# The head of a fused linear-attention and squared-ReLU kernel: 64-row transfers on a second queue and another order of the first matmuls

## The chip, the cores and the metric

The kernel runs on one core of a Trainium2 chip. The metric is the device time of one execution in microseconds (us); several runs are taken and their median is given.

## The reference

The input x has 2048 tokens of 448 features in bf16. Everything works on its layer norm. One branch is linear attention with 16 heads of 28 columns; the other is a dense layer of 1792 columns with a squared ReLU; the result is x plus their gated product.

```python
xn = _layernorm(x, axis=-1)                      # eps 1e-5
# A: linear attention
q, k, v = (xn @ wqkv) split into 16 heads of 28
phi = lambda t: jnp.where(t > 0, t + 1, jnp.exp(t)) + 1e-6
kv  = einsum("bhsd,bhse->bhde", phi(k), v)
z   = einsum("bhsd->bhd", phi(k))
o   = einsum(phi(q), kv) / (einsum(phi(q), z) + 1e-6)
s   = o @ wo
# B: squared ReLU
h = xn @ w1 + b1;  r = where(h > 0, h, 0);  out = (r * r) @ w2 + b2
return x + s * silu(out)
```

## The kernel before

The 2048 tokens are 16 tiles of 128, in 4 groups of 512. The 448 features are three full chunks of 128 rows and a rest of 64. The rest of each weight is loaded twice, into partitions 0 to 63 and 64 to 127, so that two matmuls with 64 rows each run side by side in the two halves of the array. A weight thus comes in one main transfer (`load_main`, chunks 0 to 2) and two 64-row transfers (`load_rest`, named chunk 3 and 4). w1 is cut by columns into 0 to 511 (`w10`), 512 to 1279 (`w11`) and 1280 to 1791 (`w12`), each with a main and two 64-row transfers.

The code first lists operations with what they read and write (`add`), and a planner (`schedule`, `one_pass`) then orders them. TensorE and SyncE keep the order in which the operations were listed; ScalarE, VectorE and GpSimd take what the planner's model has ready, the lowest `prio` (or latest permitted start) first, and operations with `alts` may go to another engine. The model has a duration for each operation and, for a transfer, an issue time (`dur`, 0.45) and a rate (250 bytes per ns in the first 13 us, then 330). It only decides orders; the waits in the program are semaphores. A transfer is issued by the engine that it is listed on, SyncE or ScalarE, and each engine issues one after the other.

The head is what happens before the long stream of matmuls. For each of the tiles 0 to 3: `bn_stats` (L483) and `bn_aggr` (L484) on VectorE give mean and variance, Ln and Exp on ScalarE (L491, L495) give the reciprocal standard deviation, and a tensor_scalar on VectorE (L525, for tile 0 L503 in two pieces) gives the normalized tile. TensorE transposes its three full chunks through PSUM (`pe_transpose`, L602), ScalarE or VectorE copies them to SBUF (L613, L612), and the rests of two tiles go together (`pe_transpose_rests`, L627, copied at L637) after VectorE or ScalarE has doubled the last 64 columns (`ln_twin`, L541 or L542). `k_part` (L801) multiplies a tile's three chunks with w_k, `k_rests` (L816) adds the rests of two tiles. `head_part(lo, fi)` (L829) multiplies three chunks of w1's block fi (0 or 1) with tiles lo and lo+1, and `head_rest` (L845) adds the rest and hands blocks 0 and 1 (H0.0, H0.1) over. `bias_cols` (L1234) transposes the bias b1 that `b1r` holds. `warm(n)` (L1219) issues n matmuls of 128 columns on zeros into a bank that nobody reads.

After the head the matmuls H0.2, H0.3 (columns in w10), then H0.4, H0.5 and on (L786) follow, then Q and K, the second layer G (L1109), and so on through the four groups, in an order that is written out by hand. `pe_four` runs four such units in two interleaved pairs: the first to run behind the head are the eight matmuls of H0.2 and H0.3, then those of H0.4 and H0.5, which need w11.

The squaring of the ReLU (L775 on VectorE, L776 on ScalarE) takes two blocks at a time; the ReLUs are at L764 (ScalarE) and L761 (VectorE). The normalized tiles of groups 1 to 3 are transposed on VectorE and by small transfers (`dve_transpose`), which SyncE issues and, for three of group 1, ScalarE.

Of the kernel before, what the change touches and what calls it, by code (L numbers as in the profile page):

```python
# [46 lines left out]
class Program:  # L47
# [6 lines left out]
    def add(self, eng, emit, reads=(), writes=(), dur=0.2, alts=(), nbytes=0, mode=None, label="", slow=1.0):  # L54
        op = Op(eng, emit, reads, writes, dur, alts, nbytes, mode, label)
        op.slow = slow
        for t in op.reads:
            op.raw.add(self.writer[t])
            self.readers.setdefault(t, []).append(op)
        for t in op.writes:  # L60
            w = self.writer.get(t)
            if w is not None and w is not op:
                op.deps.add(w)
            for r in self.readers.get(t, ()):
                if r is not op:
                    op.deps.add(r)
            self.writer[t] = op
            self.readers[t] = [r for r in self.readers.get(t, ()) if r is op]
        op.raw.discard(op)
        op.deps |= op.raw  # L70
        for d in op.deps:
            d.succ.append(op)
        self.ops.append(op)
        return op
# [23 lines left out]
    def one_pass(self):  # L98
# [50 lines left out]
        while n:  # L149
# [76 lines left out]
            if op.nbytes:  # L226
                free[e] = st + op.dur
                s2 = max(dma_free, st + 1.0)
                dma_free = s2 + op.nbytes * op.slow / (250e3 if s2 < 13.0 else 330e3)
                op.end = max(dma_free + 0.45, st + 1.8)  # L230
            else:
                op.end = st + du
                free[e] = op.end
                if e == "pe":
                    last_mode = op.mode
# [70 lines left out]
def bass_recurrent_scan__linear_attn_block__dense_activation_squared_relu__prompt_kernel(  # L306
    nc, A_x, A_wqkv, A_wo, B_x, B_w1, B_b1, B_w2, B_b2, out
):
    with ExitStack() as es:
# [115 lines left out]
        def dma(eng, dst, src, writes, nbytes, reads=(), dur=0.45, slow=1.0):  # L425
            return add(
                eng, lambda e, _: e.dma_start(dst, src), reads, writes, dur, nbytes=nbytes, label="dma" + str(writes[0]), slow=slow  # L427
            )

        def load_x(lo, hi, eng="sp"):  # L430
            dma(eng, x_tok[:, lo:hi, :], tiles(A_x, lo, hi), [("x", i) for i in range(lo, hi)], (hi - lo) * P * D * 2)

        def load_main(eng, w, src, name, lo, hi, c0=0, c1=3, off=0):
            dma(
                eng, w[:, c0:c1, lo:hi],
                src[128 * c0 : 128 * c1, off + lo : off + hi].rearrange("(c p) j -> p c j", p=P),
                [(name, c) for c in range(c0, c1)], 128 * (c1 - c0) * (hi - lo) * 2,
            )

        def load_rest(eng, w, src, name, lo, hi, off=0):  # L440
            for i in (0, 1):
                dma(
                    eng, w[64 * i : 64 * i + 64, 3, lo:hi], src[384:448, off + lo : off + hi], [(name, 3 + i)],
                    64 * (hi - lo) * 2,
                )

        wn = lambda name: [(name, i) for i in range(5)]
        HA = 2
        cuts = (0, 4 * P, 10 * P, F)
        load_x(0, 1)  # L450
        load_x(1, 2, "act")
        load_x(2, 4)
        load_main("sp", w_k, A_wqkv, "wk", 0, D, 0, 1, off=D)
        load_main("sp", w_k, A_wqkv, "wk", 0, D, 1, 3, off=D)
        load_rest("sp", w_k, A_wqkv, "wk", 0, D, off=D)
        dma("act", b1r[:, :], B_b1.rearrange("(f p) -> f p", p=P), ["b1r"], F * 2)
        for n, (lo, hi) in enumerate(zip(cuts, cuts[1:])):
            load_main("sp", w_1, B_w1, f"w1{n}", lo, hi)
            load_rest("sp", w_1, B_w1, f"w1{n}", lo, hi)
            if n == 1:  # L460
                load_x(4, 8)
        load_main("sp", w_q, A_wqkv, "wq", 0, D)
        load_rest("sp", w_q, A_wqkv, "wq", 0, D)
        add("act", lambda e, _: e.preload_act_table_set("natural_log_exp_and_others"), [], ["actw"], 1.3, label="table").prio = 1e6
        late_constants()

        def late_loads():
# [11 lines left out]
        def hp(si, k):  # L479
            return None if si > 3 else 5 * si + k - 25  # L480

        def ln_stats(si):
            add("dve", lambda e, _: e.bn_stats(st6[:, si, :], x_tok[:, si, :]), [("x", si)], [("st", si)], 0.61, label=f"bn{si}").prio = hp(si, 0)  # L483
            add("dve", lambda e, _: e.bn_aggr(mv[:, si, :], st6[:, si, :]), [("st", si)], [("mv", si)], 0.16, label=f"ag{si}").prio = hp(si, 1)  # L484

        def ln_rstd(lo, hi):
            c = slice(lo, hi)
# [7 lines left out]
                "act", lambda e, _: e.activation(out=rstd[:, c], in_=vep[:, c], func=AF.Exp, scale=-0.5),  # L495
                [("vep", i) for i in ts], [("rstd", i) for i in ts], 0.2, label=f"rs{lo}",
            ).prio = -40 + lo if hi - lo == 1 else None

        def ln_norm_first(si):
            for lo, hi, names in ((0, P, [("xf", si)]), (P, D, [("xn", si)])):  # L500
                add(
                    "dve",
                    lambda e, _, lo=lo, hi=hi: e.tensor_scalar(  # L503
                        out=xn[:, si, lo:hi], in0=x_tok[:, si, lo:hi], scalar1=mv[:, si, 0:1],
                        scalar2=rstd[:, si : si + 1], op0=ALU.subtract, op1=ALU.mult,
                    ),
                    [("x", si), ("mv", si), ("rstd", si)] + ([("xf", si)] if lo else []), names, 0.2 if lo == 0 else 0.33,
                    label=f"xn{si}.{lo}",
                ).prio = hp(si, 3 if lo == 0 else 4)

        def xn_cols(si, lo, hi):
            if si < 4 * SWAP:
# [81 lines left out]
        def pe_transpose(si, pieces):  # L594
            for lo, hi, eng in pieces:
                b = Buf("T")

                def f(e, _, lo=lo, hi=hi, b=b):
                    v = ps(b)[:, :].bitcast(bf)
                    last = None  # L600
                    for c in range(lo, hi):
                        last = e.transpose(v[:, (c - lo) * P : (c - lo + 1) * P], xn[:, si, c * P : (c + 1) * P], ident[:, :])  # L602
                    return last

                src = ("xf" if (si, hi) == (0, 1) else "xn", si)
                add("pe", f, [src, "ident"], [b], 0.0558 * (hi - lo), mode="128", label=f"T{si}.{lo}")

                def ev(e, eng, lo=lo, hi=hi, b=b):
                    src = ps(b)[:, 0 : 64 * (hi - lo)].bitcast(bf)
                    dst = xT[:, si, lo:hi, :].rearrange("p c k -> p (c k)")  # L610
                    if eng == "dve":
                        return e.tensor_copy(dst, src)  # L612
                    return e.activation(out=dst, in_=src, func=AF.Copy)  # L613

                n = hi - lo
                add(
                    eng, ev, [b], [("xT", si, c) for c in range(lo, hi)],
                    0.15 + 0.07 * n if eng == "dve" else 0.18 + 0.107 * n, label=f"eT{si}.{lo}",
                ).prio = -30
# [178 lines left out]
        def k_part(si, lo, hi):  # L798
            def f(e, _):
                for c in range(lo, hi):  # L800
                    last = e.matmul(  # L801
                        ps(k_head[si])[:, 0:D], xT[:, si, c, :], w_k[:, c, :], start=(c == 0), stop=False, skip_group_check=True
                    )
                return last

            add(
                "pe", f, [("wk", c) for c in range(lo, hi)] + [("xT", si, c) for c in range(lo, hi)] + ([k_head[si]] if lo else []),
                [k_head[si]], (hi - lo) * MM(D), mode="128", label=f"K{si}.{lo}",
            )
# [403 lines left out]
        def warm(n, after=()):  # L1213
            b = Buf("W")

            def f(e, _):
                last = None
                for _i in range(n):
                    last = e.matmul(ps(b)[:, 0:P], dum[:, 0:P], dum[:, 0:P], start=True, stop=True)  # L1219
                return last  # L1220

            add("pe", f, ["dum", *after], [b], n * 0.075, mode="128", label="warm")

        for i in range(4):
            ln_stats(i)
            ln_rstd(i, i + 1)
            (ln_norm if i else ln_norm_first)(i)
            if i % 2:
                ln_twin(i - 1, i + 1)

# [5 lines left out]
            )  # L1236
            add("act", lambda e, _: e.activation(out=b1f[:, :], in_=ps(bb)[:, 0 : NF // 2].bitcast(bf), func=AF.Copy), [bb], ["b1f"], 0.2, label="b1f")

        warm(35)
        warm(7, [("mv", 0)])  # L1240
        pe_transpose(0, ((0, 1, "act"), (1, 3, "dve")))
        k_part(0, 0, 1)
        warm(4)
        k_part(0, 1, 3)
        pe_transpose(1, ((0, 3, "act"),))
        warm(6)
        pe_transpose(2, ((0, 3, "dve"),))
        k_part(1, 0, 3)
        pe_transpose_rests(0)
        bias_cols()  # L1250
        head_part(0, 0)
        head_part(0, 1)
        pe_transpose(3, ((0, 3, "act"),))
        k_rests(0)
        pe_transpose_rests(2)
        head_part(2, 0)
        head_part(2, 1)
        head_rest(0)


        def ln(lo, hi):
            for si in range(lo, hi):
# [122 lines left out]
```

## Time and profile before

| | |
|---|---|
| median of 3 runs | 146.56 us (146.54 to 146.73) |
| the profiled execution | 147.21 us, span from first to last instruction 145.0 us |
| granted clock of TensorE | 1.00 over the span |
| TensorE, matmuls | 140.3 us busy, 97% of the span |
| VectorE | 102.2 us, 70% |
| ScalarE | 80.2 us, 55% |
| GpSimd | 6.6 us, 5% |
| chain that ended last | TensorE 88%, DMA 4%, SyncE's issues 4%, VectorE 1% |
| transfers | 12.89 MB, mean 89 GB/s; SyncE's queue 11.46 MB, ScalarE's 1.25 MB |

Busy times come from a profile of one execution. A busy TensorE is one whose matmuls overlap in the pipeline; its pace is read from the distance between starts. In the views, PE is TensorE, PEld its weight loads, DVE VectorE, ACT ScalarE, POOL GpSimd, SP SyncE; a q behind the engine marks its sequencer, which issues transfers. L427 is the line that issues every transfer, so transfers are told apart by the tensors that they name: `w` stands for w_1 and w_2. The time to landing is counted from the start of the issue.

### The profile page before, as it was taken

Reading aid. Unit: us, or ns where it says so; the run is one execution under the profiler, and the core shown is the slowest. Engines: PE = TensorE matmul, PEld = TensorE weight load, DVE = VectorE, ACT = ScalarE, POOL = GpSimd, SP = SyncE. Lnnn points to the kernel's source line nnn. Section 1 sums busy time; section 2 is a strip of 40 time slices with the busy share of each in tenths; the row PEclk is TensorE's granted clock in tenths of the full one; section 3 lists DMA queues with packets and bytes.
Section 4 is the critical chain, followed back from the end, with each engine's and each line's share of the span. In section 5 each row is a group of like instructions: output and inputs, shape, how many; then the busy total and the mean of one; then the engine's idle time right before and its main releaser. Section 6 shows DMA issues by size and latency. Waiting matters only on the chain.

```text
span 145.0 us, 3036 instructions
## 1 busy us (share of the span) xinstructions
PE 140.3 (97%) x1195; PEld 70.9 (49%) x1195; DVE 102.2 (70%) x222; ACT 80.2 (55%) x148; POOL 6.6 (5%) x40
## 2 busy tenths in 40 slices
PE   7998999999999999999999999999999999999991
PEld 7763444554444444444444444444547455555471
DVE  1945998889588799859778888962033736874874
ACT  3468897113688717597878468888328340302311
POOL 7900000000000000000000000000000000000000
PEclk9999999999999999999999999999999999999999
DMA  4799996469232100132100000000497000323032
GB/s 146 219 236 307 281 346 149 70 176 265 38 49 43 25 0 5 27 54 46 22 0 0 0 0 5 0 0 18 136 206 171 3 5 17 100 73 99 32 119 71
DMA packets 23515, 12.89 MB, mean 89 GB/s; under 512 B 14290, under 2 KB 22734, under 8 KB 23502
## 3 DMA queue, kind: packets, MB, share of 16 engines
q1 hardware_dynamic: 21842, 11.46, 31.0%
q10 hardware_dynamic: 1660, 1.25, 3.8%
q8 instruction: 9, 0.15, 0.4%
q14 instruction: 4, 0.03, 0.1%
HBM read 9.23 MB, written 1.90 MB: 77 GB/s over the span
## 4 chain that ended last, share of the span: by engine, by line
PE 88%; DMA 4%; SPq 4%; DVE 1%; issue 0%
PE pb L786 28%; PE pb L1109 19%; PE pb L1092 7%; PE pb L1184 7%; PE pb L887 6%; PE pb L729 6%; PE pb L739 6%; DMA w<-in_B_w_dram 4%; SPq L427 4%; PE pb L1149 3%; PE pb L866 1%; DVE gbuf L1173 1%; PE pb L893 1%; PE pb L1036 1%; PE pb L961 1%; PE pb L1062 1%
## 5 line engine op out<-in xcount | busy, mean ns | idle before, releaser
L786 PE MATMUL pb<-xT,w 64*128 64x512 bf16 x378 | 43.8, 377 | 0.5 <-DMA w<-in_B_w_dram 0.5
L764 ACT ACTIVATE r<-pb,b1f 128x512 bf16<-128x512 f32 x39 | 25.3, 685 | 16.1 <-PE pb L786 16.0
L786 PEld LDWEIGHTS pb<-xT,w 64*128 64x128 bf16 x378 | 18.0, 94 | 23.3 <-issue 1.1
L1109 PE MATMUL pb<-w,r 128*128 128x448 bf16 x140 | 27.7, 353 | 0.0
L1109 PEld LDWEIGHTS pb<-w,r 128*128 128x128 bf16 x140 | 13.1, 98 | 13.9 <-issue 1.2
L776 ACT ACTIVATE r<-r 128x1024 bf16<-128x1024 bf16 x17 | 17.8, 1061 | 0.7 <-DVE r L761 0.5
L761 DVE TENSOR_SCALAR r<-pb,b1f 128x512 bf16<-128x512 f32 x17 | 12.4, 744 | 6.0 <-PE pb L786 6.0
L1082 DVE TENSOR_TENSOR gbuf<-pb,b2b 128x448 bf16<-128x448 f32 x14 | 8.5, 617 | 5.6 <-PE pb L1109 4.1
L1204 DVE TENSOR_TENSOR gbuf<-pb,gbuf 128x448 bf16<-128x448 f32 x14 | 8.1, 618 | 6.1 <-PE pb L1184 6.1
L1092 PE MATMUL pb<-w,r 64*128 64x448 bf16 x112 | 11.8, 350 | 0.0
L729 PE MATMUL pb<-w_k,xT 64*128 64x448 bf16 x98 | 11.6, 349 | 0.0
L483 DVE BATCH_NORM_STATS2 st<-x_tok 128x6 f32<-128x448 bf16 x16 | 9.2, 609 | 3.2 <-DMA x_tok<-in_A_x_dram 3.2
L739 PE MATMUL pb<-xT,w_q 64*128 64x512 bf16 x84 | 11.0, 376 | 0.0
L1132 ACT ACTIVATE gbuf<-gbuf 128x448 bf16<-128x448 bf16 x14 | 7.0, 570 | 6.8 <-DVE gbuf L1082 5.9
L1184 PE MATMUL pb<-w_k,pqT 64*128 64x448 bf16 x96 | 10.6, 349 | 0.0
L1000 DVE TENSOR_TENSOR pqT<-pqT,xT 128x2048 bf16<-128x2048 bf16 x3 | 3.7, 1221 | 8.4 <-DMA xT<-scr 8.4
L887 PE MATMUL pb<-pk,xn 128*128 128x448 bf16 x48 | 9.6, 353 | 0.0
L719 DVE SCALAR_TENSOR_TENSOR pk<-pb,pk 128x448 bf16<-128x448 f32 x16 | 9.3, 616 | 0.1
L923 DVE TENSOR_TENSOR zacc<-zacc,pk 128x448 f32<-128x448 f32 x13 | 8.1, 620 | 0.2
L707 ACT ACTIVATE pk<-pb 128x448 bf16<-128x448 f32 x16 | 7.8, 545 | 0.6 <-PE pb L729 0.6
L1092 PEld LDWEIGHTS pb<-w,r 64*128 64x128 bf16 x112 | 5.4, 94 | 5.3 <-issue 0.4
L719 DVE SCALAR_TENSOR_TENSOR pqT<-pb,pqT 128x512 bf16<-128x512 f32 x12 | 7.7, 681 | 0.0
(99 smaller groups left out, 140.2 us busy)
## 6 DMA issues: line engine op xcount, KB each, us to landing
out_dram<-gbuf SPq DMA_DIRECT2D x15, 112.0 KB, 1.7
w<-in_B_w_dram SPq DMA_DIRECT2D x1, 1568.0 KB, 9.9
x_tok<-in_A_x_dram SPq DMA_DIRECT2D x3, 448.0 KB, 6.5
xT<-gbuf SPq DMA_DIRECT2D x32, 32.0 KB, 2.0
w<-in_B_w_dram SPq DMA_DIRECT2D x2, 384.0 KB, 5.9
xT<-scr SPq DMA_DIRECT2D x6, 112.0 KB
w<-in_B_w_dram SPq DMA_DIRECT2D x1, 576.0 KB, 6.6
xT<-scr ACTq DMA_DIRECT2D x5, 112.0 KB
```

Source lines behind the costliest of these rows:

```text
L483: add("dve", lambda e, _: e.bn_stats(st6[:, si, :], x_tok[:, si, :]), [("x", si)], [("st", si)], 0.61, label=f"bn{si}").prio = hp(si, 0)
L719: lambda e, _: e.scalar_tensor_tensor(out=slot, in0=ps(buf)[0:rows, 0:n], scalar=1.0 + 1e-6, in1=slot, op0=ALU.add, op1=ALU.max),
L729: return e.matmul(ps(b)[:, 0:D], x_tile(rows, si, c), w_k[rows, c, :], start=start, stop=stop)
L739: return e.matmul(ps(b)[:, 0:512], w_q[rows, c, m * P : (m + 1) * P], x_group(rows, g, c), start=start, stop=stop,)
L761: return e.tensor_scalar(out=slot, in0=ps(b)[:, 0:512], scalar1=b1f[:, fi : fi + 1], scalar2=0.0, op0=ALU.add, op1=ALU.max)
L764: return e.activation(out=slot, in_=ps(b)[:, 0:512], func=AF.Relu, bias=b1f[:, fi : fi + 1])
L776: return e.activation(out=both, in_=both, func=AF.Square)
L786: return e.matmul(ps(b)[:, 0:512], w_1[rows, c, fi * P : (fi + 1) * P], x_group(rows, g, c), start=start, stop=stop,)
L887: last = e.matmul(ps(b)[:, 0:D], xn_cols(si, c * P, (c + 1) * P), pk[:, si, :], start=(si == 0), stop=(si == NT - 1),)
L1092: return e.matmul(ps(b)[:, 0:D], r_cols(rows, fi, si), w_2[rows, fi, :], start=start, stop=stop)
L1109: last = e.matmul(ps(b)[:, 0:D], r_cols(slice(0, P), fi, si), w_2[:, fi, :], start=(fi == 0), stop=(fi == NF - 1),)
L1184: return e.matmul(ps(b)[:, 0:D], w, msb[rows, c, :], start=start, stop=stop)
```

## The change

- The planner's rate of the first 13 us is 280 instead of 250, and a 64-row transfer's issue time in the model is 0.58 instead of 0.45.
- x tile 1 is issued by SyncE, behind tile 0, not by ScalarE.
- w_k's main part is one transfer instead of two. Its two 64-row transfers are issued by ScalarE.
- Of w10's two 64-row transfers the first is issued by ScalarE. The bias b1r is issued by SyncE, behind w10, not by ScalarE.
- ScalarE's table load comes first on its engine, ahead of the transfers.
- `bn_aggr` of tiles 0 and 1 gets a higher priority, so that each follows its own `bn_stats`.
- The first tile is normalized whole; `ln_norm_first` is gone.
- The listed order of the first matmuls, with their dummy matmuls and the engines that copy the transposed tiles, is another.

```diff
-                dma_free = s2 + op.nbytes * op.slow / (250e3 if s2 < 13.0 else 330e3)
+                dma_free = s2 + op.nbytes * op.slow / (280e3 if s2 < 13.0 else 330e3)
...
         def load_rest(eng, w, src, name, lo, hi, off=0):
             for i in (0, 1):
                 dma(
-                    eng, w[64 * i : 64 * i + 64, 3, lo:hi], src[384:448, off + lo : off + hi], [(name, 3 + i)],
-                    64 * (hi - lo) * 2,
+                    eng if isinstance(eng, str) else eng[i], w[64 * i : 64 * i + 64, 3, lo:hi], src[384:448, off + lo : off + hi], [(name, 3 + i)],
+                    64 * (hi - lo) * 2, dur=0.58,
                 )
...
         load_x(0, 1)
-        load_x(1, 2, "act")
+        load_x(1, 2)
         load_x(2, 4)
-        load_main("sp", w_k, A_wqkv, "wk", 0, D, 0, 1, off=D)
-        load_main("sp", w_k, A_wqkv, "wk", 0, D, 1, 3, off=D)
-        load_rest("sp", w_k, A_wqkv, "wk", 0, D, off=D)
-        dma("act", b1r[:, :], B_b1.rearrange("(f p) -> f p", p=P), ["b1r"], F * 2)
+        load_main("sp", w_k, A_wqkv, "wk", 0, D, off=D)
+        load_rest("act", w_k, A_wqkv, "wk", 0, D, off=D)
         for n, (lo, hi) in enumerate(zip(cuts, cuts[1:])):
             load_main("sp", w_1, B_w1, f"w1{n}", lo, hi)
-            load_rest("sp", w_1, B_w1, f"w1{n}", lo, hi)
+            load_rest(("act", "sp") if n == 0 else "sp", w_1, B_w1, f"w1{n}", lo, hi)
+            if n == 0:
+                dma("sp", b1r[:, :], B_b1.rearrange("(f p) -> f p", p=P), ["b1r"], F * 2)
             if n == 1:
                 load_x(4, 8)
...
-        add("act", lambda e, _: e.preload_act_table_set("natural_log_exp_and_others"), [], ["actw"], 1.3, label="table").prio = 1e6
+        add("act", lambda e, _: e.preload_act_table_set("natural_log_exp_and_others"), [], ["actw"], 1.3, label="table").prio = -1e6
...
-            add("dve", lambda e, _: e.bn_aggr(mv[:, si, :], st6[:, si, :]), [("st", si)], [("mv", si)], 0.16, label=f"ag{si}").prio = hp(si, 1)
+            add("dve", lambda e, _: e.bn_aggr(mv[:, si, :], st6[:, si, :]), [("st", si)], [("mv", si)], 0.16, label=f"ag{si}").prio = hp(si, 1) if si > 1 else si - 29
...
-        def ln_norm_first(si):
...
-                src = ("xf" if (si, hi) == (0, 1) else "xn", si)
-                add("pe", f, [src, "ident"], [b], 0.0558 * (hi - lo), mode="128", label=f"T{si}.{lo}")
+                add("pe", f, [("xn", si), "ident"], [b], 0.0558 * (hi - lo), mode="128", label=f"T{si}.{lo}")
...
-            (ln_norm if i else ln_norm_first)(i)
+            ln_norm(i)
...
-        warm(35)
-        warm(7, [("mv", 0)])
-        pe_transpose(0, ((0, 1, "act"), (1, 3, "dve")))
-        k_part(0, 0, 1)
+        warm(31)
+        warm(9, [("mv", 0)])
+        pe_transpose(0, ((0, 3, "act"),))
+        warm(7)
+        pe_transpose(1, ((0, 3, "dve"),))
+        k_part(0, 0, 3)
+        pe_transpose_rests(0)
+        k_part(1, 0, 3)
+        head_part(0, 0)
+        pe_transpose(2, ((0, 3, "dve"),))
+        head_part(0, 1)
+        k_rests(0)
         warm(4)
-        k_part(0, 1, 3)
-        pe_transpose(1, ((0, 3, "act"),))
-        warm(6)
-        pe_transpose(2, ((0, 3, "dve"),))
-        k_part(1, 0, 3)
-        pe_transpose_rests(0)
+        pe_transpose(3, ((0, 3, "dve"),))
         bias_cols()
-        head_part(0, 0)
-        head_part(0, 1)
-        pe_transpose(3, ((0, 3, "act"),))
-        k_rests(0)
         pe_transpose_rests(2)
+        warm(4)
         head_part(2, 0)
         head_part(2, 1)
         head_rest(0)
```

More of the change, by code (lines that the diff above doesn't have):

```diff
@@ L497, in ln_rstd @@
             ).prio = -40 + lo if hi - lo == 1 else None
-        def ln_norm_first(si):
[L500 to L509, printed above, removed]
         def xn_cols(si, lo, hi):
```

## The prediction

> **What bounds the kernel now.** I read the chain of waits first, because it says which stretch sets the end. Its columns are start, length (both us), and what the chain passes through.
>
> ```profile
> 6.36 0.50 SPq L427
> 6.90 6.17 DMA w<-in_B_w_dram
> 13.07 0.05 issue
> 13.11 8.38 PE pb L786 x76
> ...
> 136.54 4.30 PE pb L1149 x28
> 140.87 0.43 DVE gbuf L1162
> ```
>
> Up to 6.90 us the chain is SyncE issuing one transfer after the other; then it is the flight of the second 64-row piece of w1's columns 512 to 1279, which lands at 13.07; from 13.11 to 140.87 it is TensorE without a break. So everything that precedes 13.11 counts only by when H0.4, the first matmul that needs those columns, can start. The waits of TensorE from 13 us to 141 us confirm it: one entry.
>
> ```profile
> PE pb L786 <- DMA w<-in_B_w_dram: 0.5, 1, 0.5
> ```
>
> The third view is the timeline of the head (start, length, engine, what, xcount, idle before).
>
> ```profile
> 0.81 0.86 SPq L427 DMA_DIRECT2D x_tok<-in_A_x_dram  x2
> 1.05 4.66 PE L1219 MATMUL pb<-dum 128*128 128x128 bf16 x42 [1.05 <-DVE dum L368]
> 1.26 0.67 ACTq L427 DMA_DIRECT2D b1r<-in_B_b_dram  x1
> 1.96 1.28 ACT L464 ACT_TABLE_LOAD   x1 [1.96 <-issue]
> 4.70 0.29 ACT L491 ACTIVATE vep<-mv,eps 128x1 f32<-128x1 f32 x1 [1.46 <-DVE mv L484]
> 5.64 0.79 PE L602 MATMUL pb<-ident,xn 128*128 128x128 bf16 x3
> 7.37 0.50 PE L1219 MATMUL pb<-dum 128*128 128x128 bf16 x6
> 8.55 0.39 DVE L525 TENSOR_SCALAR xn<-x_tok,mv,rstd 128x448 bf16<-128x448 bf16 x1
> 10.05 0.49 ACT L613 ACTIVATE xT<-pb 128x384 bf16<-128x384 bf16 x1 [0.58 <-PE pb L602]
> 10.60 0.83 PE L829 MATMUL pb<-xT,w 128*128 128x256 bf16 x6
> 11.58 1.03 PE L786 MATMUL pb<-xT,w 64*128 64x512 bf16 x8
> ```
>
> A second limit lies close behind the transfer. The head matmuls of tiles 2 and 3 (L829) start at 10.60, H0.2 follows at 11.58 and is through at 12.61: from 10.60 to where H0.4 could begin are 2.01 us. An earlier transfer alone therefore gains at most 0.50 us; more needs the chain through the four tiles to move too.
>
> The table by half microseconds (length, busy time of PE, PEld, DVE, ACT, POOL, clock, share of the DMA engines, GB/s) says how full the DMA engines are while that chain runs.
>
> ```profile
> 4.00:4.50 0.50, 0.50 (x8) 0.50 (x6) 0.47 (x2) 0.00 (x0) 0.50 (x6) 1.00 0.80 151
> 5.50:6.00 0.50, 0.42 (x4) 0.10 (x1) 0.46 (x3) 0.19 (x2) 0.50 (x3) 1.00 0.53 99
> 8.00:8.50 0.50, 0.50 (x5) 0.28 (x5) 0.22 (x1) 0.47 (x3) 0.00 (x0) 1.00 0.91 101
> ```
>
> At 5.5 they ran half empty: w1's first piece was issued only at 3.92. At 8.0 they were busy but slow: waiting data, not a missing issue.
>
> **The change part by part. The transfers.** In SyncE's queue ahead of the last piece of the second cut of w1, the change removes one of w_k's two main issues (0.48 with its gap), its two 64-row issues (0.62, 0.63) and one of w1's (0.54), and adds x tile 1 (0.46) and the bias b1r (0.67 and a gap on ScalarE, say 0.65 here). Net 2.27 - 1.11 = 1.16 us earlier: 6.90 becomes 5.74. If the landing follows the issue it comes at 11.9. If it follows only the filling of empty DMA time, the table gives the gain: the unfilled shares of the six slices from 3.5 to 6.5 (0.85, 0.80, 0.89, 0.77, 0.53, 0.74) come to 1.42 slices, 0.71 us, so 12.36. The two slow slices at 8.0 stay in both. The pessimistic end is the one starved slice alone, 0.47 x 0.5 = 0.24 us: 12.8. I take 12.1, between the first two, since both starved time and a late issue are visible in the rows.
>
> **ScalarE.** The table moves to 0.8 and ends at 2.1; three 64-row issues follow. Rows for an issue go from 0.42 to 0.67, so they end near 4.0 (3.4 to 4.2). Behind them wait Ln and Exp of tile 0, and behind these the normalization, the transpose and all of the head. bn_stats of tile 0 can start when x lands (0.81 + 2.3 = 3.1) and takes 0.59; with aggregation at once (0.17) the statistics are there at 3.9, against 4.6 when both tiles' bn_stats went first. So Ln starts at about 4.05 instead of 4.70, and the normalized tile, 0.57 us after Ln's start plus 0.42, is there at 5.05. The issues hide under the statistics of tile 0; without that cover each further 0.1 us of issuing would cost 0.1. The other engine's issues can stretch one: where ScalarE issued beside SyncE at 24.4, one SyncE issue took 1.21 instead of 0.61. With three ScalarE issues that long Ln would start at 5.8. From Ln to the second L829 were 5.9 us: shifted whole, 11.7, and the kernel 0.6 slower. But VectorE can do a bn_stats (0.59) in that wait, and T3 stood 0.7 us behind the first Ha, from 8.94 to 9.68, so I get 10.4 to 10.7 and a gain of 0.3 to 0.5 left.
>
> **VectorE.** Removed: the split of the first normalization (0.71 becomes 0.42) and the evacuation of half of tile 0 (0.29). Added: evacuations of tiles 1 and 3 (0.36 each; ScalarE did them in 0.49). Its list up to the normalization of tile 3 was 5.5 us of work from 3.30 and ended at 8.94. Now it is 5.5 - 0.29 - 0.29 + 0.36 = 5.3 from 3.1, with 0.2 more if the copy of the last columns comes here: 8.6 to 9.0 with the same small waits.
>
> **TensorE.** The first 42 dummy matmuls have a pitch of 0.106 us ((4.66 - 0.31) / 41), the six at 7.37 one of 0.056: its clock came up at about 6.3. The new order has 40 dummies, to 1.05 + 40 x 0.106 = 5.3, so T0 starts at 5.3 and not when its tile is ready; before 5.63. Then, at the slow pitch, T0 and 7 dummies (10 x 0.107): 6.4. At the fast one T1 0.17, three K matmuls of tile 0 at 0.19, two rests 0.2, K of tile 1 0.57: 7.9, with up to 0.4 for the evacuation of T1 in this sum or beside it. Ha0 (3 x 0.11), T2 0.2, Ha1 0.33, K rests 0.25, four dummies 0.22: 9.3, and T3 0.17: 9.5. w1's first cut must be there at 8.0; it landed at 8.2 from 3.92 and is now issued at about 2.6. The result of T3 passes to VectorE and back: 0.28 for the matmul's end and the semaphore, 0.36, 0.1: Ha0 for tiles 2 and 3 at 10.25. b1r's transpose, the rests and four dummies fit beside that. 10.25 + 2.01 = 12.26 for H0.4.
>
> **Sum.** H0.4 starts at the later of 12.1 and 12.3: 12.3 against 13.11, a gain of 0.8 us. Behind it nothing seems to turn late. The second half of G0's sum starts 26.9 and the last squaring ends 24.1; w2 lands at 22.7 and G0 starts 24.3; the transposed second group is in SBUF by about 31.5 and H1 starts at 35.0. Each has over 1.5 us. The profiled execution took 147.21 us (span 145.0 and 2.2 around it) and becomes 146.4; the median of the runs, 146.56, lies 0.65 below that execution, so 145.8.
>
> **The rivals.** *The transfers come hardly earlier.* One set of 16 DMA engines serves both queues; if only the starved slice is filled, w1 lands at 12.8 and the gain is 0.3: 146.3. For it: the slices at 8.0, slow at a full share. Against: the starvation from 3.5 to 6.0. The Trainium skill (DMA: Bandwidth & Descriptors, Issuing engines are not separate DMA queues) says that issuing from several engines saves only the sequencer's issue time. By that rule the result is this rival or the 1.16 us of the issues, as the issue or the data binds; the trace shows both, one after the other.
>
> *Both limits come better.* If TensorE's clock comes up by 5.3 rather than 6.3, the ten slow matmuls cost 0.5 less, H0.4 could start at 11.75, and w1 at 11.9 binds: gain 1.2, 145.3.
>
> *Slower: the clock comes up later.* The change replaces the run of 42 by 40 dummies and puts T1, which waits for a normalized tile, ahead of all K work. If TensorE idles there before 6.3 and stays at the slow pitch, the 2.9 us of work that I counted from 6.4 to 9.3 takes up to twice as long. Half of it slow is 1.45 us: H0.4 at 13.75, 0.65 late, 147.2; all of it, 148.7. It decides from 0.8 us of such lag. Against it: in the trace the clock came up although TensorE had been idle for 0.2 to 0.4 us just before T0's pieces. The Trainium skill (TensorE: Matmul & The Clock Gate, Part 1) states that a free-running window of about 3.4 us must be busy for the clock to be released; the trace's 5.2 us from the first matmul to the fast pitch does not contradict that.
>
> *The gain is given back.* The change also alters the planner's rate and issue lengths, so the order on ScalarE and VectorE and the choice between them may differ anywhere. One or two stalls of 0.4 us would return it: 146.6. The trace before has none behind 13.11, so any would be new.
>
> **How the numbers follow.** Forecast 0.52, transfers hardly earlier 0.16, both better 0.14, clock later 0.12, given back 0.06. About 0.2%, 0.3 us, is what a measurement can tell from no change. Faster: 0.50 + 0.14 + 0.06 of the first rival = 0.70; same: 0.02 + 0.08 + 0.03 = 0.13; slower: 0.12 + 0.02 + 0.03 = 0.17. The range runs from 145.1, a little under the better case, to 147.0, which leaves out most of the slow-clock case; the forecast's own range is 145.3 to 146.2.
>
> **What would show it.** Right: H0.4 at 12.0 to 12.6, its waiting time under 0.3 us, the last 64-row piece of w1's second cut issued near 5.7, and L829's second group near 10.25. Wrong in the transfers: that piece lands after 12.6. Wrong on ScalarE: Ln of tile 0 after 4.5. Wrong on the clock: dummies or K matmuls at the 0.1 pitch after 6.5. Given back: any TensorE wait behind the start of the stream. The forecast as a whole fails if the span from H0.4 to the end is no longer 131.9 us.

## The result and the profile after

| | before | after |
|---|---|---|
| median of 6 runs | 146.64 us (146.54 to 147.10) | 146.11 us (145.96 to 146.18) |
| ratio after to before | | 0.9958 [0.9945, 0.9972] |
| the profiled execution | 147.21 us, span 145.0 | 146.12 us, span 144.0 |
| span, median of the runs of each kernel | 145.1 us | 144.0 us, in ten further runs 144.25 |
| time less span | 1.78 us | 2.07 us, in the ten further runs 2.04 |

The change makes the kernel 0.3 to 0.55% faster. Forecast were 145.8 us and "faster" with 0.70. The last two rows are read from the list of runs, which gives the time and the span of each; those of before are medians over the runs of the kernel before that lay beside the experiments. They matter below. In five of ten executions of one kernel below (main transfers first), and in one each of three others, the granted clock fell to a mean of 0.988 and the time was 1.6 to 3.4 us longer; medians and ratios leave these executions out.

**The chain that ended last**, of the kernel after (start, length, what it passes through):

```profile
1.06 4.45 PE pb L1206 x40
5.51 0.32 PE pb L590 x3
...
10.40 0.73 PE pb L816 x6
11.13 0.32 PE pb L832 x2
11.45 9.06 PE pb L773 x84
...
135.57 4.30 PE pb L1136 x28
139.89 0.43 DVE gbuf L1149
```

Line numbers have moved: L1206 are the dummy matmuls, L590 the transposes, L816 and L832 the head matmuls, L773 the stream H, L788 and L803 the K matmuls, L513 the normalization. Before, this view began with SyncE's issues and the flight of w1's last piece. Now TensorE holds the chain from 1.06 on, and no transfer is on it. The waits of TensorE say the same: the entry L786 <- w is gone, and only the start of the program is left.

```profile
PE pb L1206 <- DVE dum L368: 1.1, 1, 1.1
```

**The timeline of the head** (start, length, engine, what, xcount, idle before):

```profile
0.80 1.28 ACT L464 ACT_TABLE_LOAD   x1 [0.80 <-PEq L1356]
0.84 1.23 ACTq L427 DMA_DIRECT2D w_k<-in_A_wqkv_dram  x2
...
3.77 0.30 ACT L491 ACTIVATE vep<-mv,eps 128x1 f32<-128x1 f32 x1 [1.69 <-DVE mv L484]
...
5.23 0.63 DVE L483 BATCH_NORM_STATS2 st<-x_tok 128x6 f32<-128x448 bf16 x1 [0.46 <-DMA x_tok<-in_A_x_dram]
5.30 0.53 PE L590 MATMUL pb<-ident,xn 128*128 128x128 bf16 x3
...
9.04 0.39 DVE L513 TENSOR_SCALAR xn<-x_tok,mv,rstd 128x448 bf16<-128x448 bf16 x1
...
10.30 0.83 PE L816 MATMUL pb<-xT,w 128*128 128x256 bf16 x6
...
11.29 3.40 PE L773 MATMUL pb<-xT,w 64*128 64x512 bf16 x30
```

The last row holds H0.2 to H0.4 and on without a gap. Its matmuls start in pairs every 0.215 us, so H0.4, the fifth pair, starts at 11.29 + 4 x 0.215 = 12.15. Before it was 13.11. The 0.96 us split into two: the head matmuls of tiles 2 and 3 start at 10.30 instead of 10.60 (0.30), and from there to H0.4 pass 1.85 us instead of 2.51 (0.66), because w1 is there. From H0.4 to the end it is 131.85, against 131.9 before: nothing behind was won or lost.

**The half microseconds that were starved or slow before** (length, busy PE, PEld, DVE, ACT, POOL, clock, DMA share, GB/s), and the transfer of w1's last piece of the second cut:

```profile
4.00:4.50 0.50, 0.50 (x8) 0.50 (x6) 0.47 (x3) 0.27 (x2) 0.50 (x6) 1.00 0.87 276
5.50:6.00 0.50, 0.50 (x8) 0.50 (x6) 0.50 (x2) 0.14 (x1) 0.50 (x5) 1.00 0.85 256
8.00:8.50 0.50, 0.50 (x7) 0.41 (x6) 0.13 (x2) 0.38 (x3) 0.00 (x0) 1.00 1.02 366
```

```profile
w<-in_B_w_dram SPq DMA_DIRECT2D x1, 96.0 KB, 5.3
```

At 5.5 the DMA engines moved 99 GB/s and now 256; at 8.0 it was 101 and now 366. The last piece is issued at 5.83 (6.90 before) and lands 5.3 us later, at 11.11, so it is issued 1.07 earlier and lands 1.96 earlier.

### The profile page after: what moved, and what is told of

Its sections match the earlier page's. It is cut to its first block, busy times and chain, and to the rows that moved or that the text cites. A ratio compares the mean times of both kernels' runs of the same rounds, so it can differ in the third digit from the quotient of the medians.

```text
span 144.0 us, 3040 instructions
## 1 busy us (share of the span) xinstructions
PE 140.0 (97%) x1198; PEld 71.4 (50%) x1198; DVE 103.8 (72%) x225; ACT 77.4 (54%) x143; POOL 6.4 (4%) x40
## 4 chain that ended last, share of the span: by engine, by line
PE 96%; DVE 2%; issue 0%
PE pb L773 29%; PE pb L1096 19%; PE pb L1079 7%; PE pb L1171 7%; PE pb L874 6%; PE pb L716 6%; PE pb L726 6%; PE pb L1206 4%; PE pb L1136 3%; PE pb L853 1%; DVE gbuf L1160 1%; PE pb L880 1%; PE pb L816 1%; PE pb L788 1%; PE pb L1023 1%; PE pb L948 1%
## 5 line engine op out<-in xcount | busy, mean ns | idle before, releaser
L773 PE MATMUL pb<-xT,w 64*128 64x512 bf16 x378 | 43.6, 376 | 0.0
L773 PEld LDWEIGHTS pb<-xT,w 64*128 64x128 bf16 x378 | 18.0, 94 | 22.6 <-issue 1.1
L763 ACT ACTIVATE r<-r 128x1024 bf16<-128x1024 bf16 x15 | 15.7, 1062 | 0.4 <-DVE r L748 0.3
L762 DVE TENSOR_TENSOR r<-r 128x1024 bf16<-128x1024 bf16 x13 | 8.4, 685 | 0.2
```

The lines of the kernel that those rows point to most:

```text
L763: return e.activation(out=both, in_=both, func=AF.Square)
L773: return e.matmul(ps(b)[:, 0:512], w_1[rows, c, fi * P : (fi + 1) * P], x_group(rows, g, c), start=start, stop=stop,)
```

## The experiments

The theory: the issues bind. SyncE's queue of issues held back w1, two queues bring it earlier, and the new order on the engines must keep up. Against it stood that the bytes bind and not the issues, and that the order alone brings the gain while the transfers do nothing. The ratio is always to the kernel before, run on the same chip at the same time.

**The kernel before once more** (no edit), for the half microsecond by which its profiled execution lay above its median.

> The kernel before once more, unchanged. The two spans differ by 1.0 us (145.0 and 144.0), the medians of the times only by 0.53. Theory A: the profiled execution of before was an unlucky one, in which w1's second cut met the slow slices around 8.0 us. Then this execution lands w1's last piece at about 12.4 to 12.7, H0.4 starts at 12.4 to 12.7 and the span is 144.4 to 144.6. Theory B: the slow slices come in every execution. Then w1 lands at 13.0 to 13.1, the span is again 145.0, and the missing half microsecond lies outside the span. Ratio to before 1.000 in both.

Ratio 0.9999 [0.9972, 1.0025], median 146.97 us, spans from 144.5 to 146.1 us. In this profile w1 landed at 12.81, between what the two theories expected, and the chain ran elsewhere:

```profile
0.81 2.68 DMA x_tok<-in_A_x_dram
...
10.35 0.50 ACT xT L613
```

It starts with x tile 1, which landed at 3.49, and reaches the second L829 at 10.89, 0.29 later than in the first profile. This view hides that w1 was still the last to come. The row in which H0.4 begins shows it:

```profile
12.31 1.15 PE L786 MATMUL pb<-xT,w 64*128 64x512 bf16 x8
```

Eight matmuls in four pairs take 1.03 us when nothing holds them (L786 at 11.58 in the first profile) and here 1.15. The pairs start at 12.31, 12.53, 12.86 and 13.09; the late one is H0.4, at 12.86, 0.05 after the landing. So in the kernel before the transfer ended last in both profiles, by 0.67 us in the first (reckoned below) and by 0.11 in the second, with the tiles' chain close behind. Part of the half microsecond lay outside the span: 2.2 us there in the first profiled execution, 1.78 as a rule.

**The transfers alone.** The old listing of orders is kept; transfers, table load and the planner's rates are those of the change. The planner then orders ScalarE and VectorE anew, so these two do not keep the orders of the kernel before.

```diff
-        load_x(1, 2, "act")
+        load_x(1, 2)
-        load_rest("sp", w_k, A_wqkv, "wk", 0, D, off=D)
+        load_rest("act", w_k, A_wqkv, "wk", 0, D, off=D)
...
```

> The change's transfers alone (both queues, x tile 1 and b1r on SyncE, the table first, the planner's new rate); aggregation, first normalization and order of the first matmuls as before. Theory 'both limits': w1's last piece lands near 11.1 as after the change and binds no longer, the second L829 starts at 10.6 as before, H0.4 at 10.6 + 1.84 = 12.44. Span 144.3, that is 0.3 longer than after the change; against before 0.1 to 0.3 us faster in the median if theory A holds, 0.67 if B. Rival 'the transfers do it all': span 144.0 to 144.1, as after the change.

Ratio 1.0042 [1.0023, 1.0061], median 147.55: slower, where both theories had it faster. w1's last piece did land at 10.96, as in the kernel after. The loss lies ahead of it:

```profile
2.22 4.37 DMA w_k<-in_A_wqkv_dram
6.59 0.04 issue
6.64 0.36 PE pb L801
...
7.81 0.49 ACT xT L613
8.30 0.19 ACT vep L491
...
11.84 0.83 PE pb L829 x6
```

w_k's main part, now one transfer, lands at 6.59; its first chunk alone had landed at 4.54. The old order wants K of tile 0 first and TensorE waits 0.6 us for it, T1 stands behind it, and the second L829 comes at 11.84 instead of 10.60. That w_k is the cause is argued from this chain; two experiments below try to take this wait away, the second does, and it gains 0.1 us. By the span the loss is 0.4 us (145.5 against 145.1); the time less the span, 2.05 instead of 1.78, adds the rest.

**The order alone.** The change's listing and priorities with the old transfers.

```diff
-        load_rest("act", w_k, A_wqkv, "wk", 0, D, off=D)
+        load_rest("sp", w_k, A_wqkv, "wk", 0, D, off=D)
...
+        load_x(1, 2, "act")
```

> The change without its transfers: aggregation tile by tile, first tile normalized whole, the new order of the first matmuls; SyncE's and ScalarE's transfers, the table's place and the planner's rate as before. Theory 'both limits': w1's last piece lands where before has it (12.4 to 13.1), H0.4 waits for it, no gain: ratio 0.999 to 1.002. Rival 'the order does it all': H0.4 at 12.2, span 144.0, ratio 0.996.

Ratio 1.0038 [1.0012, 1.0065], median 147.42. No gain, so the order alone is not the cause; that it is even slower was not expected. The chain holds the reason for its profiled execution:

```profile
6.92 7.11 DMA w<-in_B_w_dram
14.03 0.09 issue
14.12 1.02 PE pb L773 x7
```

w1 was issued as in the kernel before and landed 0.96 later; TensorE waited 1.0 us for it. The DMA engines were at a share of 0.70 to 0.83 from 4 to 9 us. Why the same queue took so long here is open. This profile is a long one of its kernel (span 146.0, median 145.35). By the median span the order alone loses only 0.25 us; another 0.28 lies outside the span (2.06 instead of 1.78).

**One queue.** The change, but with the 64-row pieces back on SyncE.

```diff
-        load_rest("act", w_k, A_wqkv, "wk", 0, D, off=D)
+        load_rest("sp", w_k, A_wqkv, "wk", 0, D, off=D)
...
-            load_rest(("act", "sp") if n == 0 else "sp", w_1, B_w1, f"w1{n}", lo, hi)
+            load_rest("sp", w_1, B_w1, f"w1{n}", lo, hi)
```

> The kernel after, but w_k's two 64-row transfers and w1's first one go back to SyncE's queue; the rest as after. Three issues of 0.6 us come ahead of w1's second cut: its last piece is issued at 5.83 + 1.85 = 7.7. Theory 'the issue binds': it lands 1.85 later than after the change, at 12.9 to 13.0, H0.4 waits for it, span 144.8, ratio to before 1.000 to 1.003. Theory 'the data binds' (one set of DMA engines, only issue time is saved): w1's first cut comes later, but the second lands by 12.0 and the span stays within 0.2 of 144.0. x tiles 2 and 3, which land at 5.21 after the change and 4.29 before, should come back to 4.3 or earlier in both.

Ratio 0.9981 [0.9953, 1.001], median 146.75. The last piece was issued at 7.34 and landed at 13.04:

```profile
7.34 5.70 DMA w<-in_B_w_dram
13.04 0.09 issue
```

H0.2 started at 11.39, so H0.4 could have started at 11.39 + 0.86 = 12.25; it started at 13.13, as expected where the issues bind. Not every execution is like this: in three of the ten the span was 144.1 to 144.5 us, as after the change, so one queue can bring w1 in time but as a rule does not. The table by microseconds shows the low rates of the kernel before again, at a share of 0.83 from 5 to 6 us and of 0.48 from 8 to 9:

```profile
5.00:6.00 1.00, 1.00 (x12) 1.00 (x11) 0.97 (x4) 0.24 (x2) 1.00 (x7) 1.00 0.83 104
...
8.00:9.00 1.00, 0.84 (x9) 0.67 (x9) 0.13 (x1) 0.50 (x2) 0.00 (x0) 1.00 0.48 129
```

**One queue, main transfers first.** All on SyncE, the same number of issues, the six 64-row pieces behind the main transfers and b1r.

```diff
+        first = [find("x", 0), find("x", 1), find("x", 2), find("wk", 0), find("w10", 0), b1, find("w11", 0)]
+        first += [find(n, c) for n in ("wk", "w10", "w11") for c in (3, 4)]
+        pr.order["sp"] = first + [o for o in pr.order["sp"] if o not in first]
```

> One queue, all on SyncE, with the 64-row transfers behind the main ones: x, w_k, w1's first cut, b1r, w1's second cut, and then the six 64-row pieces; orders on the other engines as after the change. Number and size of the transfers are those of the one-queue kernel with pairs in place, whose w1 landed at 13.04. Theory 'issues bind': what matters is that bulk is issued ahead of the engines; w1's second main part is issued near 3.9 instead of 6.4, the slow stretches of 5 to 9 us go, w1's last piece lands by 11.6, and the span is 144.0 to 144.4 (the K rests may wait for w_k's pieces until 9.5). Theory 'two queues': one queue alone keeps the slow stretches, w1 lands after 12.3, span over 144.6.

The same last piece, issued at the same 7.34, landed at 11.64 instead of 13.04, and the slices are full:

```profile
5.00:6.00 1.00, 0.85 (x14) 0.67 (x13) 0.97 (x4) 0.54 (x2) 1.00 (x7) 1.00 1.10 341
...
8.00:9.00 1.00, 0.47 (x6) 0.18 (x3) 0.78 (x3) 0.04 (x1) 0.00 (x0) 1.00 0.99 208
```

This separates issues from bytes most clearly: bytes, queue and number of issues are those of the run above, and only the small pieces no longer stand ahead of the big ones. It is one profile of each, and the landing varies between executions, but all profiles agree: in the four in which all pieces of w_k and of w1's first cut stand ahead on SyncE (the kernel before twice, the order alone, one queue) w1's last piece landed at 12.81 to 14.03, in the nine others, without the merged transfers below, at 10.96 to 12.70. What leaves the DMA engines short of work is, by these rows, an issue time of 0.4 to 0.6 us spent on 56 to 96 KB; the 104 GB/s at a share of 0.83 are not explained by it. The Trainium skill (DMA: Bandwidth & Descriptors, Issuing engines are not separate DMA queues) says that further issuing engines save only this issue time; the trace agrees, one engine fills the DMA engines as well when it issues large transfers first. The section adds that this time is usually small beside the transfer. Beside the 2.4 us and more that these pieces take to land it is. It is not beside the 0.17 to 0.29 us that their 56 to 96 KB would fill at the 341 GB/s of the row above, an estimate.

As a kernel it is no better. The pieces of w_k came at 10.24 and 10.48, and the K rests waited for them:

```profile
7.98 0.49 PE L816 MATMUL pb<-xT,w 128*128 128x256 bf16 x3
10.57 0.53 PE L803 MATMUL pb<-w_k,xT 64*128 64x448 bf16 x2 [2.10 <-DMA w_k<-in_A_wqkv_dram]
...
12.63 1.49 PE L816 MATMUL pb<-xT,w 128*128 128x256 bf16 x6
```

Ratio 0.998 [0.9963, 0.9996]. The profiled execution, with a span of 147.0 us, is one in which the clock fell. The last row shows it: six matmuls of 256 columns take 1.49 us, with a pitch of 0.213 us instead of 0.109. The granted clock was 0.82 from 10 to 11 us and 0.50 from 11 to 14. It is the harm that the rival "the clock comes up later" had in mind, here behind an idle time of 2.1 us that the change itself does not have.

**Fewer issues on one queue.** A pair of 64-row transfers becomes one transfer of 128 rows that reads the 64 source rows twice.

```diff
+            twice = ap(src, [[0, 2], [row, 64], [1, hi - lo]], 384 * row + off + lo)
+            dma(eng, w[:, 3, lo:hi], twice, [(name, 3), (name, 4)], P * (hi - lo) * 2)
```

> One queue again, all on SyncE, but each pair of 64-row transfers is one transfer of 128 rows that reads the 64 rows twice; orders on the other engines as after the change. Issues ahead of w1's second cut shrink by three, its last one comes near 5.6 (7.34 with one queue and pairs, 5.83 after the change). Theory 'issues bind': SyncE's issue slots, 0.6 us each for little data, starve the DMA engines; with fewer issues one queue does as well as two: w1's last piece lands at 11.0 to 11.5, span 143.9 to 144.2, times as narrow as after the change. Theory 'two queues': the engines are only full when both queues have work; then the slow starts of 5 to 9 us stay, w1 lands after 12.3 and the span is 144.4 to 145.5, with a wide spread.

Ratio 1.0598 [1.0517, 1.068], median 155.71. It failed for a reason of its own and tells nothing about issues or bytes. 112 KB for w_k, issued at 2.66, landed at 8.16, and b1r behind it took from 4.53 to 12.46:

```profile
10.00:11.00 1.00, 1.00 (x12) 0.49 (x9) 0.80 (x3) 0.43 (x1) 0.00 (x0) 1.00 0.14 45
```

A share of 0.14 is about 2 of 16 engines, and only two engines reported the end of each such transfer. The Trainium skill (DMA: Bandwidth & Descriptors, Why a DMA increments its semaphore by 16 and not by 1) states that the number of engines is the largest one up to 16 that divides the slowest dimension of both sides; the source's slowest dimension here is the 2 of the repetition. The trace agrees.

**x tiles 2 and 3 first on ScalarE's queue**, with the rest of the change kept, since VectorE waited 0.46 us for them.

```diff
+        x2 = next(o for o in pr.order["sp"] if o.label == "dma('x', 2)")
+        pr.order["sp"].remove(x2)
+        pr.order["act"].insert(1, x2)
```

> The kernel after, with x tiles 2 and 3 issued by ScalarE as the first of its transfers instead of third on SyncE; all orders on the other engines unchanged. These tiles landed at 5.21 after the change and VectorE waited 0.46 for them; now they land by 4.2 and the wait goes. Theory 'TensorE's own list binds' (dummies, slow pitch up to 6.5, then w1's first cut at 8.0): T3 stays at 9.5, span 144.0, ratio to before as after the change, 0.996. Rival 'VectorE's chain binds': T3 and all behind come 0.3 to 0.45 earlier, span 143.6.

Ratio 0.995 [0.9926, 0.9974], median 146.21, spans 143.8 to 144.7. They land at 3.85 instead of 5.21, but x tile 0 at 3.59 instead of 2.87, so VectorE waits there instead. The second L816 is at 10.03, 0.27 earlier, but the x tiles need not be the reason: T1 starts at 6.38 as after the change (6.37), runs at the fast pitch here (three matmuls 0.34 against 0.45), and K of tile 0 follows at 6.55 instead of 6.82. The median time is about that of the kernel after. w1's last piece was issued at 5.09, 0.74 earlier than after the change, and landed at 11.25, no earlier.

**The same with fewer dummy matmuls**, five before T0 and three before T3.

```diff
-        warm(31)
+        warm(31, real=26)
...
-        warm(4)
+        warm(4, real=1)
```

> As the kernel with x tiles 2 and 3 on ScalarE, and five dummies fewer ahead of T0 and three fewer ahead of T3; all orders otherwise unchanged. Theory 'TensorE's own list binds': T0 starts at 4.8 instead of 5.3, but K of tile 0 waits for w_k (landed 6.7) and the first Ha for w1's first cut (8.0), so only the three dummies ahead of T3 count: T3 at 9.3, span 143.8. Rival 'the clock': with fewer dummies TensorE's fast pitch comes later than 6.6 and the span grows by 0.3 or more.

Ratio 0.9929 [0.9907, 0.9952], median 145.88, spans 143.8 to 144.4. The clock did not come later in the profile: T0, at 5.42, is fast (three matmuls 0.34). But when the fast pitch begins changes between executions of one kernel: T0 of the kernel after is slow at 5.30 in its first profile (0.53) and fast at 5.15 in its second (0.33). One profile therefore cannot rule this rival out. The second L816, at 10.08, is no earlier than with all the dummies. It is the lowest median of all, but the interval overlaps that of the kernel after run again (below): better by 0.2 to 0.4 us, or the same; these runs can't tell.

**w_k's main part in two again**, on top of the transfers alone, to give K of tile 0 its chunk early.

```diff
+        load_main("sp", w_k, A_wqkv, "wk", 0, D, 0, 1, off=D)
+        load_main("sp", w_k, A_wqkv, "wk", 0, D, 1, 3, off=D)
```

> The transfers alone (orders of before), which was slower, with w_k's main part cut into chunk 0 and chunks 1 to 2 as before. Theory 'w_k holds the old order': there K of tile 0 stands ahead of T1, w_k as one transfer landed at 6.59, and T1, its copy, Ln of tile 2 and all behind came late. Cut in two, chunk 0 lands near 5.7, K starts near 6.3, and the span falls from 145.6 to about 145.2. Rival 'x tiles 2 and 3 hold it' (they landed at 5.32): span unchanged at 145.5.

Ratio 1.0053 [1.0029, 1.0077], median 147.96: a miss. The further issue pushed chunks 1 and 2 to 7.30, and the wait moved to them.

**K of tile 0 behind T1**, also on top of the transfers alone: the one step of the new order that I took for the cure.

```diff
+        late, t1 = pe[k0 : k0 + 3], pe[k0 + 3]
+        pe[k0 : k0 + 4] = [t1] + late
```

> The transfers alone with the orders of before, but K of tile 0 (with its dummies) moved behind T1 on TensorE; nothing else differs from the transfers-alone kernel (span 145.6). Theory 'w_k holds the old order': T1 no longer waits for w_k, its copy and Ln of tile 2 come about 1 us earlier, and the span falls to 144.4 to 144.9. Rival: the old order loses by something else (evacuations on ScalarE, the late aggregation of tile 1); span 145.3 or more.

Ratio 1.0043 [1.003, 1.0057], median 147.48, span 145.4 against 145.5: another miss, and the useful one. The wait for w_k alone is not what makes the transfers alone slow. With it off the path the chain shows what lay behind it:

```profile
5.72 0.28 ACT xT L613
6.00 0.19 ACT vep L491
...
6.45 0.46 DVE xn L525
...
7.25 0.55 DVE st L483
...
11.69 0.83 PE pb L829 x6
```

Ln of tile 1 stands behind the copy of transposed tile 0 on ScalarE and starts only at 5.89 in the timeline; in the kernel after it starts at 4.50. The whole chain of four tiles follows it. And bn_stats of tile 2, which ran at 4.65 in the kernel before, runs only at 7.16 here, behind the normalization of tile 1, though its tile had landed at 5.85. The rows point to ScalarE's and VectorE's order as what the second half of the change repairs (aggregation tile by tile, and another engine for the copies); which of its lines does most was not tried, nor were the new transfers with exactly the orders that the kernel before had on these two engines.

**The kernel after once more** (no edit).

> The kernel after once more, beside the next three. If what it gains is steady, the ratio to before is 0.994 to 0.997 again, the spans lie within 143.9 to 144.3, and w1's last piece lands before H0.4 could start (12.15).

Ratio 0.996 [0.9937, 0.9982], median 146.30, spans 143.9 to 144.7. This profile shows the next limit:

```profile
1.72 4.12 DMA x_tok<-in_A_x_dram
5.84 0.02 issue
5.86 0.63 DVE st L483
6.49 0.31 DVE xn L513
```

x tiles 2 and 3 landed at 5.84 here; bn_stats of tile 2 follows and, as VectorE's list has it, the normalization of tile 1 stands behind it, so T1 comes at 6.84 and TensorE idles 1.0 us.

**x tile 1 first on ScalarE's queue and fewer dummies**, meant to beat both kernels.

```diff
+        x1 = next(o for o in pr.order["sp"] if o.label == "dma('x', 1)")
+        pr.order["sp"].remove(x1)
+        pr.order["act"].insert(1, x1)
```

> A version meant to beat both: the kernel after, with x tile 1 back on ScalarE as its first transfer, so that tile 0 comes at 3.1, tile 1 at 3.3, tiles 2 and 3 at 4.3 and VectorE does not wait, and with five dummies fewer ahead of T0 and three fewer ahead of T3. Orders otherwise as after. T1 at 6.2, w1's first cut at about 7.7 sets the first Ha, T3 at 9.2: span 143.6 to 143.8, ratio to before 0.993. If tile 0 still lands after 3.4, as with tiles 2 and 3 on ScalarE, the span is 143.8 to 144.0.

Ratio 0.9959 [0.9938, 0.998], median 146.22: no better. In its profile w_k's main part landed at 7.62 and K waited 1.0 us. w1's last piece, issued at 5.07, landed at 12.12. With the change the issues seem to bind no longer: issued at 5.83, 5.84, 5.09, 5.08 and 5.07 (the kernel after twice and these three variants), it landed at 11.11, 11.71, 11.25, 11.45 and 12.12.

**What follows.** Each half of the change loses 0.4% alone, and both together win 0.4%. By the median span the halves lose 0.4 and 0.25 us and both win 0.85 to 1.1. The new transfers bring w1 earlier, by 1.96 us in the first pair of profiles and 1.1 in the second, but w_k's first chunk and x tiles 2 and 3 later; with the orders that the planner makes of the old listing the tiles then come too late to use it. The new orders reach H0.4 early, but with the old transfers w1 isn't there. Which of the new orders matter is argued from the rows only.

## Why the prediction was right, and where its steps were off

The forecast was 0.8 us earlier for H0.4, by TensorE's list at 12.3 and not by w1; H0.4 came at 12.15, by TensorE's list. Sign and mechanism held in the profiled execution. In the second profile H0.4 came at 12.57, and there the landing of x tiles 2 and 3 and VectorE behind it set the time, so that TensorE's list is the limit in some executions only. Step by step:

- **Issues.** The last piece at 5.74 was forecast; it was 5.83.
- **w1's landing was mis-sized.** 12.1 was taken, between 11.9 and 12.8; it was 11.11 (11.71 in the second profile). The step kept the two slow slices at 8.0 "in both", as waiting data. They were no fixed feature: from 8.0 to 8.5 the rate was 101 GB/s in the first profile of the kernel before, 223 in its second, 366 after the change. So even the best end of the range, "landing follows issue" at 11.9, was too late. What makes a busy DMA engine slow there isn't shown. It did no harm, as w1 was not what bound.
- **"From 10.60 to where H0.4 could begin are 2.01 us" was mis-sized.** It added the end of the last matmul of H0.2. Ends overlap: each matmul is shown with 0.376 us, the pairs start every 0.215. Four pairs from 11.58 end the list at 12.44, so the distance was 1.84, and TensorE's stall was 0.67 and not 0.50; an earlier transfer alone could thus have gained 0.67. This makes 12.26 into 12.09; measured were 12.15.
- **Ln of tile 0** at 4.05 was forecast; it was 3.77. The table load and the issues were added up. The rows show them at the same time: the load from 0.80 to 2.08, the first two issues from 0.84 to 2.07, all three done at 2.71 and not at 4.0. Ln then waited for the statistics alone, which came at 3.74, as x tile 0 landed at 2.87 and not at 3.1. No issue of SyncE took twice its time beside them.
- **VectorE's list** should have ended at 8.6 to 9.0; it ended at 9.43. x tiles 2 and 3 landed at 5.21 instead of 4.29, because ScalarE's 64-row pieces now stand ahead of them (with these back on SyncE they landed at 4.39), and VectorE waited 0.46. No step had asked what the pieces issued early take from x. It cost nothing in the profiled execution, where T3 came at 9.52 (9.5 forecast); in the second profile they landed at 5.84, T1 waited for VectorE, and the second L816 came 0.42 later, at 10.72.
- **TensorE's list.** T0 at 5.3: 5.30. Second head matmuls at 10.25: 10.30. T1 still ran at the slow pitch of 0.107, which the step had fast, and K of tile 0 followed at 6.82, fast. The clock rival did not occur in either profile; as the start of the fast pitch changes between executions (see the fewer dummies), that is in part luck.
- **Given back.** No wait of TensorE behind the start: right.
- **The sum was too large by what lies outside the span.** It took the time less the span as unchanged. By the medians of the runs the span gained 0.85 to 1.1 us, and the time less the span grew from 1.78 to 2.04 or 2.07: 0.26 to 0.29 us came back. That is nearly all of the 0.3 us between 145.8 and 146.11. No line of the two profiles shows why. By kernel it was 1.73 to 1.76 with everything on SyncE, 1.86 to 1.89 in the variants where ScalarE's first transfer is an x tile, 2.04 to 2.08 where it is a piece of w_k. But the kernel before, whose ScalarE also begins with an x tile, had 1.78, and the order alone, with the same transfers, 2.06; these fit no such rule. It stays open.

## What to carry to other kernels

A transfer that is late may be late because of what is issued ahead of it: where the share of the DMA engines falls while transfers wait to be issued, put large transfers first or give the small ones to another engine, and look at what they then push back. Before costing a change in two parts, ask of each whether it gains without the other; here neither did. Where a planner orders the engines, an experiment on the transfers alone changes these orders too; hold them fixed to tell the two apart. And compare time less span between kernels, since a gain in the profile is not all of it a gain in time.

## What the runs showed of the hardware

- ScalarE issues transfers while its table loads: two issues (0.84 to 2.07) lie wholly inside the 1.28 us of the load (0.80 to 2.08).
- A transfer whose source repeats 64 rows by an outer dimension of 2 ran on two engines: 5.5 us for 112 KB (issued at 2.66, landed at 8.16).
- TensorE's clock fell to half behind an idle time of 2.1 us (main transfers first), at 10.6 us, and was back at 14.1. The Trainium skill (TensorE: Matmul & The Clock Gate, Part 1) names an idle window of about 3.4 us for this; here 2.1 us sufficed in the profiled execution, and the measurement decides. The length of the wait is not the whole of it: in the kernel with merged transfers the clock stayed full over 3.12 us of idle (up to 18.09) and fell at 33.7, behind a wait of 2.51 us that ended at 32.52, until 37.1. Both low stretches lasted 3.4 us.
- Time less span differed by up to 0.35 us (1.73 to 2.08) between kernels whose edits concern only the first microseconds.
